# Clearing block buffers between weight casts, reordering chunk loads, moving the first casts to VectorE and taking four turns of q and k one product later in a fused retention and gated feed-forward kernel

## The chip, the cores and the metric

The kernel runs on one core of a Trainium2 chip. The metric is the device time of one execution in microseconds (us), the median of several executions. The profile's span is shorter than that time by about 1.8 us (335.2 against 336.99 us for the profiled execution of the kernel before). Engines are named as in the profile: PE (TensorE), PEld (its weight loads), DVE (VectorE), ACT (ScalarE), POOL (GpSimd), SP (the queue that issues the DMAs).

## The reference

```python
scores = scale * np.matmul(q, k.transpose(0, 1, 3, 2))      # batch 8, heads 8, sequence 576, head 64
Dmat = np.where(rel >= 0, gamma[:, None, None] ** rel[None, :, :], 0.0)
ret = scores * Dmat[None, :, :, :]
attn = np.matmul(ret, v)
x = attn.transpose(0, 2, 1, 3).reshape(B * S, H * D)        # 4608 tokens x 512
out = (sigmoid(x @ w_gate) * (x @ w_val)) @ w_out           # hidden 1536
```

The decay splits into a factor for the row and a factor for the column. The kernel multiplies q and k by tables of these while it casts them to bf16, and carries a running state from chunk to chunk.

## The kernel before

TensorE interleaves the retention with the feed-forward products. The first 768 columns (tokens) are done in three "pairs" of 128-row tiles; the rest is done in chunks of up to 128 rows. For a chunk, the loads are cast into buffers in block-diagonal form (zeros must surround the blocks, so each of the four buffers of each kind, `qk_nat` and `vbd`, is cleared once), and a DMA transpose turns q and k:

```python
for nm, src in (("v", v), ("k", k), ("q", q)):        # load(s): order of the three loads of a chunk
    ...
def casts_to(s):
    while done["cast"] <= min(NS - 1, s):
        x = done["cast"]
        loads_to(x + (1 if x < 12 else 2))
        cast_k(x)      # GpSimd: 4 instructions of 64x256, into qk_nat
        cast_q(x)      # GpSimd: 1 instruction of 128x512, into qk_nat
        cross(x)       # DMA transpose of qk_nat, issued by SP
        cast_v(x)      # GpSimd: 4 instructions of 64x256, into vbd
        done["cast"] += 1
```

The loads, the transposes and the stores all go through one queue, in program order. The middle of the kernel, where the weights' casts end and the chunks begin (cuts marked):

```python
    for i in range(4):
        cast_w("g", 4, 4, i, on_pool)
    step(h_both((2, 3)), 4)                 # gate and value products of feature blocks 2, 3
    ...                                     # casts and products of blocks 4 to 7, casts of 8 to 11
    for t in vbd[0:2]:
        nc.gpsimd.memset(t, 0.0)
    ...                                     # casts of w_out and of the third pair's k, q
    units = h_both((8, 9, 10, 11))
    step(units, 4)
    turn("k", 2, 0, tr_psum, "tr")          # TensorE transposes a block of k or q; ScalarE copies it out
    step(units, 1)
    cast_wo(3, on_act)
    turn("q", 2, 0, pv_psum, "pv")
    ...
    pair_qk(2, 0, QK)
    op_first((0, 1, 2), (0,), opps)         # output products
    pair_qk(2, 1, [(tr_psum, "tr"), (pv_psum, "pv")])
    nc.vector.memset(qk_nat[0], 0.0)
    nc.vector.memset(qk_nat[1], 0.0)
    op_first((0, 1, 2), (1, 2), opps)
    later_constants()                       # the causal mask, GpSimd
    ...
    for t in vbd[2:4]:
        nc.gpsimd.memset(t, 0.0)
    for t in qk_nat[2:4]:
        nc.vector.memset(t, 0.0)
    casts_to(1)
```

## Time and profile before

| | before |
|---|---|
| median | 337.68 us (336.75 to 338.0, 3 runs; a fourth came with the result) |
| span, granted clock | 335.2 us, 1.000 |
| PE busy | 325.7 us |
| GpSimd, ScalarE, VectorE busy | 186.4, 167.6, 165.1 us |

Busy times say who works; the chain says what the end depends on. The page gives the chain that ended last as shares of the span, by engine:

```profile
PE 76%; DMA 10%; POOL 8%; issue 2%; SPq 1%; DVE 1%; ACT 1%; POOLq 0%; DVEq 0%
```

TensorE is 97% busy and yet only 76% of this chain. For the rest, the end hangs on DMAs and on GpSimd. In order of time, the chain leaves TensorE at 25.4 us and comes back to it at 84.42 us, and no row of TensorE stands in between (cuts marked):

```profile
26.41 5.31 DMA wv<-in_moe_w_val_dram
...
40.12 5.95 DMA wo<-in_moe_w_out_dram
46.12 0.62 POOL wo_sb L230
...
79.58 4.80 DMA T<-qk_nat
84.42 0.41 PE qk L410 x8
```

So TensorE's waits between 26 and 84 us don't lie on this chain; the one at 84.42 us does.

### The profile page before, as it was taken

To read this page: it belongs to the slowest core of one execution; us is meant where nothing else is said; L and a number is where in the kernel's file an instruction comes from. 1 tells how busy PE (TensorE), PEld (TensorE's weight loads), DVE (VectorE), ACT (ScalarE), POOL (GpSimd) and SP (SyncE) were. 2 spreads that over 40 slices of the span, in tenths; PEclk is the share of its full clock that TensorE was granted. 3 is DMA by queue.
4 is the path that set the end of the run, shared out by engine and by line. 5 is a ranking of instruction groups with operands and counts; after the bars stand their busy time and mean duration, and the time that the engine had idled before them with its cause. 6 is when DMAs were issued, how large, how long until landed. Compare 5 with 4: busy or idle time off the path is not lost.

```text
span 335.2 us, 7536 instructions
## 1 busy us (share of the span) xinstructions
PE 325.7 (97%) x2836; PEld 190.0 (57%) x2868; DVE 165.1 (49%) x331; ACT 167.6 (50%) x345; POOL 186.4 (56%) x328
## 2 busy tenths in 40 slices
PE   8899999999999999999999999999999999999996
PEld 7764445969566566556566555545555455444443
DVE  5845755626376356436346635542574156503320
ACT  6555635547566456355556655445646455233321
POOL 5675679868969898882448966582577500000000
PEclk9999999999999999999999999999999999999999
DMA  7999996899999999999986999499765850020002
GB/s 215 315 369 348 341 267 128 164 189 185 189 200 186 205 195 249 188 215 225 248 136 128 192 241 198 99 192 277 143 137 80 254 203 0 2 95 31 2 31 94
DMA packets 164100, 60.00 MB, mean 179 GB/s; under 512 B 144480, under 2 KB 156000, under 8 KB 164064
## 3 DMA queue, kind: packets, MB, share of 16 engines
q1 hardware_dynamic: 163920, 59.39, 82.9%
q8 instruction: 22, 0.36, 0.5%
q10 hardware_dynamic: 144, 0.13, 0.1%
q14 instruction: 14, 0.11, 0.1%
HBM read 37.75 MB, written 9.44 MB: 141 GB/s over the span
## 4 chain that ended last, share of the span: by engine, by line
PE 76%; DMA 10%; POOL 8%; issue 2%; SPq 1%; DVE 1%; ACT 1%; POOLq 0%; DVEq 0%
PE h L506 42%; PE op L572 22%; DMA wo<-in_moe_w_out_dram 3%; POOL qk_nat L258 3%; PE pv L431 2%; PE qk L410 2%; DMA k32p<-in_k_dram 2%; PE pv L429 2%; DMA wv<-in_moe_w_val_dram 2%; DMA k<-in_k_dram 2%; POOL qk_nat L268 2%; PE st L443 1%; POOL vbd L279 1%; DMA T<-qk_nat 1%; SPq L114 1%
## 5 line engine op out<-in xcount | busy, mean ns | idle before, releaser
L506 PE MATMUL h<-xT,wg_sb 128*128 128x384 bf16 (+2 forms) x476 | 102.4, 336 | 0.4 <-DVE gv L534 0.2
L506 PE MATMUL h<-xT,wv_sb 128*128 128x384 bf16 (+2 forms) x473 | 102.2, 336 | 0.4
L258 POOL TENSOR_TENSOR qk_nat<-k,ktab 64x256 bf16<-64x256 f32 x120 | 73.5, 612 | 43.0 <-PE st L443 27.8
L534 DVE TENSOR_TENSOR gv<-g,h 128x384 bf16<-128x384 bf16 (+1 forms) x96 | 59.7, 621 | 72.1 <-PE h L506 55.7
L572 PE MATMUL op<-wo_sb,gv 128*128 128x512 bf16 x356 | 84.5, 379 | 0.8
L530 ACT ACTIVATE g<-h 128x384 bf16<-128x384 f32 (+1 forms) x96 | 52.2, 544 | 64.9 <-PE h L506 58.3
L449 DVE CAST sbd<-st 64x256 bf16<-64x256 f32 x104 | 43.7, 420 | 45.3 <-PE st L443 43.0
L506 PEld LDWEIGHTS <-wg_sb 128*128 128x128 bf16 x480 | 43.7, 98 | 31.4 <-issue 0.4
L506 PEld LDWEIGHTS <-wv_sb 128*128 128x128 bf16 x480 | 44.1, 98 | 29.0 <-issue 0.4
L279 POOL CAST vbd<-v 64x256 bf16<-64x256 f32 x120 | 47.6, 397 | 14.6 <-PE pv L431 6.1
L572 PEld LDWEIGHTS <-gv 128*128 128x128 bf16 x372 | 34.3, 98 | 36.3
L549 ACT COPY ob<-op 128x512 f32<-128x512 f32 x33 | 19.3, 586 | 47.0 <-PE op L572 41.4
L289 ACT CAST vs<-v 64x256 bf16<-64x256 f32 x104 | 41.9, 403 | 1.6
L268 POOL TENSOR_TENSOR qk_nat<-q,qtab 128x512 bf16<-128x512 f32 (+1 forms) x34 | 35.4, 1042 | 2.6
L433 ACT CAST xT<-pv 128x512 bf16<-128x512 f32 (+1 forms) x34 | 18.2, 534 | 18.3 <-PE pv L431 18.2
L412 DVE TENSOR_TENSOR pt<-qk,tri 128x512 bf16<-128x512 f32 (+1 forms) x34 | 21.2, 625 | 6.1 <-PE qk L410 5.8
L443 PEld LDWEIGHTS <-qk_nat 128*128 128x128 bf16 x208 | 13.2, 98 | 8.7
L431 PE MATMUL pv<-pt,vbd 128*128 128x64 bf16 x240 | 18.0, 193 | 0.0
L431 PEld LDWEIGHTS <-vbd 128*128 128x128 bf16 x240 | 15.2, 98 | 3.5
L429 PE MATMUL pv<-T,sbd 128*128 128x64 bf16 x216 | 17.2, 193 | 0.0
L522 DVE TENSOR_TENSOR gv<-g,h 128x256 bf16<-128x256 bf16 x24 | 10.0, 420 | 13.8 <-ACT g L520 13.4
L429 PEld LDWEIGHTS <-sbd 128*128 128x128 bf16 x216 | 15.1, 98 | 2.5
(80 smaller groups left out, 238.3 us busy)
## 6 DMA issues: line engine op xcount, KB each, us to landing
out_dram<-ob SPq DMA_DIRECT2D x34, 256.0 KB, 2.9
v<-in_v_dram SPq DMA_DIRECT2D x26, 256.0 KB, 4.1
k<-in_k_dram SPq DMA_DIRECT2D x26, 256.0 KB, 4.6
q<-in_q_dram SPq DMA_DIRECT2D x26, 256.0 KB, 5.0
wg<-in_moe_w_gate_dram SPq DMA_DIRECT2D x12, 256.0 KB, 5.8
wv<-in_moe_w_val_dram SPq DMA_DIRECT2D x12, 256.0 KB, 5.4
wo<-in_moe_w_out_dram SPq DMA_DIRECT2D x12, 256.0 KB, 5.4
k32p<-in_k_dram SPq DMA_DIRECT2D x6, 256.0 KB, 5.4
```

What stands on the lines that cost most here:

```text
L258: nc.gpsimd.tensor_tensor(out=kn[half(hh), j, :, half(hh)], in0=k32[half(j), hh::2, :], in1=ktab[half(j), c, hh::2].unsqueeze(2).to_broadc ...
L268: nc.gpsimd.tensor_tensor(out=qs[0:n], in0=q32[0:n], in1=qtab[0:n, c, :].unsqueeze(2).to_broadcast([n, H, D]), op=ALU.mult)
L279: nc.gpsimd.tensor_copy(out=vb[half(hh), j, :, half(hh)], in_=v32[half(j), hh::2, :])
L289: nc.scalar.copy(out=natural["vs", s][half(hh), j], in_=loaded[s][0][half(j), hh::2, :])
L412: nc.vector.tensor_tensor(out=pt[:, :, 0:n].rearrange("p m (j t) -> p m j t", t=64), in0=qkp[:, :, 0:n].rearrange("p m (j t) -> p m j t", ...
L429: nc.tensor.matmul(pvp[:, m, half(j)], lhsT=before[:, m, :], rhs=qT[:, m, half(j)], start=True, stop=False)
L431: nc.tensor.matmul(pvp[:, m, half(j)], lhsT=vb[:, j, m, :], rhs=pt[:, m, half(j)], start=before is None, stop=True)
L449: nc.vector.tensor_copy(out=sb[half(hh), :, half(hh)], in_=st_tiles[b][half(hh)])
L506: nc.tensor.matmul(out, lhsT=w_sb[:, kc, fc * P:(fc + 1) * P], rhs=xT[:, kc, t0 + a:t0 + e], start=(kc == 0), stop=(kc == NKC - 1))
L530: nc.scalar.activation(out=g[:, 0:n], in_=h1[:, 0:n], func=AF.Sigmoid)
L534: nc.vector.tensor_tensor(out=gvs[some[0]][:, a:e], in0=g[:, 0:n], in1=h2[:, 0:n], op=ALU.mult)
L572: nc.tensor.matmul(opp, lhsT=gvs[fc][:, nb * P:(nb + 1) * P], rhs=wo_sb[:, fc, :], start=(fc == 0), stop=(fc == NFC - 1))
```

## The change

The intent is to take work off GpSimd in the stretch where the first chunk's transpose is being prepared, and to stop two short waits of TensorE on the third pair's turns (a turn is a TensorE transpose of a block of q or k). It has three parts, called turns, clears and casts below:

```diff
 # casts: load order, and the first casts on VectorE
-        for nm, src in (("v", v), ("k", k), ("q", q)):
+        for nm, src in (("k", k), ("q", q), ("v", v)):
...
-            cast_q(x)
+            cast_q(x, nc.vector if x < 2 else nc.gpsimd)
             cross(x)
-            cast_v(x)
+            cast_v(x, on_dve if x == 0 else on_pool)
...
+    casts_to(0)
     cast_dense(0, 0)
 # clears: between the weight casts
+    later_constants()
     for i in range(4):
         cast_w("g", 4, 4, i, on_pool)
+    nc.gpsimd.memset(vbd[0], 0.0)
...                                  (vbd[1], vbd[2], qk_nat[0:3] likewise, further on)
-    for t in vbd[0:2]:
-        nc.gpsimd.memset(t, 0.0)
...                                  (the later clears and later_constants go)
 # turns: one product later, and one output product ahead of the first scores
     step(units, 4)
     cast_wo(2, on_pool)
+    step(units, 1)
     turn("k", 2, 0, tr_psum, "tr")
+    cast_wo(3, on_act)
     step(units, 1)
-    cast_wo(3, on_act)
     turn("q", 2, 0, pv_psum, "pv")
...
+    op_first((0,), (0,), opps)
     pair_qk(2, 0, QK)
-    op_first((0, 1, 2), (0,), opps)
+    op_first((1, 2), (0,), opps)
     pair_qk(2, 1, [(tr_psum, "tr"), (pv_psum, "pv")])
-    nc.vector.memset(qk_nat[0], 0.0)
-    nc.vector.memset(qk_nat[1], 0.0)
+    nc.vector.memset(qk_nat[3], 0.0)
+    nc.gpsimd.memset(vbd[3], 0.0)
```

More of the change, by code (lines that the diff above doesn't have):

```diff
@@ L253, in cast_k @@
         n = width[c]
-        k32 = loaded[s][1]
+        k32 = loaded[s][0]
         kn = qk_nat[s % NB][:, 1:3]
@@ L261, in cast_k, with cast_q, cast_v @@
         natural["k", s] = kn
-    def cast_q(s):
+    def cast_q(s, eng=nc.gpsimd):
         b, c = STEPS[s]
         n = width[c]
-        q32 = loaded[s][2]
+        q32 = loaded[s][1]
         qs = qk_nat[s % NB][:, 0].rearrange("p m (hh d) -> p (m hh) d", d=D)
-        nc.gpsimd.tensor_tensor(out=qs[0:n], in0=q32[0:n],
-                                in1=qtab[0:n, c, :].unsqueeze(2).to_broadcast([n, H, D]), op=ALU.mult)
-    def cast_v(s):
+        eng.tensor_tensor(out=qs[0:n], in0=q32[0:n],
+                          in1=qtab[0:n, c, :].unsqueeze(2).to_broadcast([n, H, D]), op=ALU.mult)
+    def cast_v(s, eng=on_pool):
         b, c = STEPS[s]
         n = width[c]
-        v32 = loaded[s][0]
+        v32 = loaded[s][2]
         vb = vbd[s % NB]
@@ L278, in cast_v @@
             for hh in range(2):
-                nc.gpsimd.tensor_copy(out=vb[half(hh), j, :, half(hh)], in_=v32[half(j), hh::2, :])
+                eng(out=vb[half(hh), j, :, half(hh)], in_=v32[half(j), hh::2, :])
         natural["vb", s] = vb
@@ L288, in cast_dense @@
         for hh in range(2):
-            nc.scalar.copy(out=natural["vs", s][half(hh), j], in_=loaded[s][0][half(j), hh::2, :])
+            nc.scalar.copy(out=natural["vs", s][half(hh), j], in_=loaded[s][2][half(j), hh::2, :])
     def cross(s):
@@ L740 @@
     cast_w("v", 4, 4, 3, on_dve)
+    nc.gpsimd.memset(vbd[1], 0.0)
     units = h_both((4, 5, 6, 7))
+    for t in qk_nat[0:2]:
+        nc.vector.memset(t, 0.0)
     step(units, 4)
@@ L746 @@
     cast_w("g", 8, 4, 3, on_act)
+    nc.gpsimd.memset(vbd[2], 0.0)
     step(units, 4)
@@ L757 @@
     cast_wo(1, on_dve)
+    nc.vector.memset(qk_nat[2], 0.0)
     cast_pair("q", 2, 0, nc.vector)
@@ L762 @@
     cast_wo(2, on_pool)
+    step(units, 1)
     turn("k", 2, 0, tr_psum, "tr")
+    cast_wo(3, on_act)
     step(units, 1)
-    cast_wo(3, on_act)
     turn("q", 2, 0, pv_psum, "pv")
+    cast_wo(4, on_pool)
     step(units, 1)
-    cast_wo(4, on_pool)
     turn("k", 2, 1, tr_psum, "tr")
@@ L771 @@
     turn("q", 2, 1, pv_psum, "pv")
-    step(units, 1)
     cast_wo(5, on_act)
@@ L790 @@
     opps = [ffn_psum.tile([P, 512], FP32, tag="ffn", name=f"op_0_{nb}") for nb in range(3)]
+    op_first((0,), (0,), opps)
     pair_qk(2, 0, QK)
-    op_first((0, 1, 2), (0,), opps)
+    op_first((1, 2), (0,), opps)
     pair_qk(2, 1, [(tr_psum, "tr"), (pv_psum, "pv")])
-    nc.vector.memset(qk_nat[0], 0.0)
-    nc.vector.memset(qk_nat[1], 0.0)
+    nc.vector.memset(qk_nat[3], 0.0)
+    nc.gpsimd.memset(vbd[3], 0.0)
     op_first((0, 1, 2), (1, 2), opps)
-    later_constants()
     op_first((3, 4, 5), range(3), opps)
@@ L821 @@
     store(opps[3], 3 * P, on_act)
-    for t in vbd[2:4]:
-        nc.gpsimd.memset(t, 0.0)
-    for t in qk_nat[2:4]:
-        nc.vector.memset(t, 0.0)
     casts_to(1)
```

## The prediction

> **What bounds the kernel now.** I read the shares of busy time first, then the list of what TensorE (PE) waited for, then PE's instructions in order of time around each wait, and last what VectorE (DVE), GpSimd (POOL) and the DMA issues did just before those waits.
>
> The page of the kernel before, busy time:
>
> ```profile
> span 335.2 us, 7536 instructions
> PE 325.7 (97%) x2836; PEld 190.0 (57%) x2868; DVE 165.1 (49%) x331; ACT 167.6 (50%) x345; POOL 186.4 (56%) x328
> ```
>
> PE is short of work for 335.2 - 325.7 = 9.5 us only. Its list of waits says which of that is a wait (us in total, times, longest):
>
> ```profile
> PE kTp L317 <- POOL kp L248: 1.0, 3, 0.4
> PE qk L410 <- DMA T<-qk_nat: 0.6, 2, 0.4
> PE st L351 <- ACT sbd L362: 0.6, 1, 0.6
> PE qTp L317 <- ACT qT L327: 0.4, 1, 0.4
> ```
>
> The change touches the first, second and fourth. In order of time (start, length, and in brackets the idle time that the view shows) they are these, each below the row ahead of it:
>
> ```profile
> 32.15 3.62 PE L621 MATMUL hg<-xT,wg_sb 128*128 128x512 bf16 x15
> 36.15 0.40 PE L317 MATMUL kTp<-ident,kp 128*128 128x128 bf16 x4 [0.39 <-POOL kp L248]
> ...
> 38.55 1.03 PE L621 MATMUL hv<-xT,wv_sb 128*128 128x512 bf16 x4
> 39.98 0.38 PE L317 MATMUL qTp<-ident,qp 128*128 128x128 bf16 x4 [0.40 <-ACT qT L327]
> ...
> 56.05 0.60 PE L506 MATMUL h<-xT,wv_sb 128*128 128x256 bf16 x4
> 57.08 0.41 PE L410 MATMUL qk<-T 128*128 128x64 bf16 x8 [0.43 <-DMA T<-qk_nat]
> ...
> 83.61 0.60 PE L506 MATMUL h<-xT,wv_sb 128*128 128x256 bf16 x4
> 84.42 0.41 PE L410 MATMUL qk<-T 128*128 128x64 bf16 x8 [0.21 <-DMA T<-qk_nat]
> ```
>
> The brackets understate the loss, because a row's length includes the drain of its last product, which a following product would overlap. From start to start, sixteen 512-column products take 3.45 us elsewhere (rows at 25.24 and 28.69), four take 0.86, four 256-column ones 0.435. So PE should have gone on at 32.15 + 3.45 = 35.60, 38.55 + 0.86 = 39.41, 56.05 + 0.435 = 56.49 and 83.61 + 0.435 = 84.05. It lost 0.55, 0.57, 0.59 and 0.37 us: **2.08 us in all**. These are the four places that the change can win. From 84.9 to 320 us PE shows only one more wait that is named, 0.2 us at 178.6 on a VectorE product; gaps of 0.05 "issue" are records that are missing.
>
> Why the third wait is there, from GpSimd's and the DMA queue's order of time:
>
> ```profile
> 46.12 0.62 POOL L230 CAST wo_sb<-wo 128x512 bf16<-128x512 f32 x1 [0.86 <-DMA wo<-in_moe_w_out_dram]
> 46.68 0.15 POOL L212 MEMSET tri<- 128x64 bf16 x1
> 46.90 0.52 POOL L214 TENSOR_SCALAR_AFFINE_SELECT tri<-tri 64x64 bf16<-64x64 bf16 x2
> 47.48 1.84 POOL L823 MEMSET vbd<- 128x1024 bf16 x2
> 49.41 2.66 POOL L258 TENSOR_TENSOR qk_nat<-k,ktab 64x256 bf16<-64x256 f32 x4
> 52.14 1.04 POOL L268 TENSOR_TENSOR qk_nat<-q,qtab 128x512 bf16<-128x512 f32 x1
> 53.21 1.54 SPq L295 DMA_TRANSPOSE T<-qk_nat  x1
> ```
>
> GpSimd runs without a pause from 46.12: mask, two memsets, k, q. Then the transpose goes out at 53.21 and lands 3.8 us later (that tile's view), at 57.0, where PE stands. The fourth wait is the same chain some chunks on (a k load landing, GpSimd casting to 79.5, a transpose issued at 79.58 that lands after 4.8).
>
> **What the Trainium skill says.** "Perfetto Trace Analysis", section "Identifying the Most-Contended Engine", warns that matmul busy share is no measure of headroom. The trace agrees in part: busy ends are longer than the starts' spacing (1.03 against 0.86 us above), so I used spacing. "TensorE: Matmul & The Clock Gate", "Back-to-back issue gap", gives about N/2.4 + 2.5 ns for one isolated product and 131 ns in a sustained stream at N=512. This trace has 3.45/16 = 216 ns and agrees with the isolated form, so PE is streaming at its rate and only waits can be won. "VectorE: DVE Perf Modes", "Zero memsets can be issued as uint32 (trn2)", counts one cycle per element; the buffer clears are indeed 128x768 uint32 here, 0.70 us each. "SBUF — State Buffer", "SBUF: two separate sides", says that VectorE and GpSimd lock a shared pair of ports for whole instructions. The trace fits: a VectorE weight cast at 33.17 takes up to 1.28 us, beside a GpSimd memset, against 0.43 for the same form at 27.04.
>
> **The change part by part.** No product and no byte is added or removed; PE's work stays the same.
>
> *Clears between weight casts.* GpSimd's three vbd clears (0.92 us each, half of 1.84) and the mask (0.15 + 0.52 = 0.67) go to 22 to 31 us. There GpSimd waits 0.7 to 0.8 us before most casts for weights to land, so they mostly fill idle time. By my replay from the landing times (issue time plus time to landing), the second v weight cast of feature blocks 4 to 7 ends at about 27.2 instead of 27.0, and PE's use of it starts at 28.69; the later casts catch up by 31 us. After the last w_out cast (46.74) only one clear is left, so k can start at 46.7 + 0.9 = 47.7 instead of 49.4.
>
> *VectorE.* Two qk_nat clears (1.4 us) fall between 27.5 and 29.0, where VectorE idles 2.36 us before 29.82; the third falls at about 34.3 to 35.0, ahead of a q load that lands at 35.6. All are hidden. The clears at 53.2 (1.50) go away, which pays for the casts that VectorE takes over.
>
> *Turns one product later.* The k turn now comes after the first v product, at 35.60 + 0.86 = 36.46, and k is ready at 36.10 (start 34.88 + 1.22): the 0.55 is gone. The ScalarE copy that frees the bank for the last q turn still stands behind a w_out cast that waits for its DMA: 38.68 + 0.62 = 39.30, + 0.73 = about 40.0. PE comes to that turn after three more products and three turns of about 0.3: 36.46 + 3 x 0.86 + 3 x 0.3 = 39.9. So the 0.57 shrinks to about 0.1. The next wait could be the pair's second half of scores, which needs that last turn copied (two copies, to about 41.3); I put PE there at 41.3, since one output product has been moved ahead of the first half. I allow 0.1 more. **Gain about 0.9 us.**
>
> *k, q, v and VectorE's casts.* k takes the slot in which v was issued (40.83 + 6.3 = 47.1), q the next (41.54 + 6.8 = 48.3), v the third (42.45 + 7.0 = 49.5). GpSimd casts k from 47.7 to 50.4. VectorE casts q after its last state copy (before at 49.78, about 0.9 earlier now), so 49.3 to about 50.2, at 0.75 to 1.04 for that form. The transpose leaves at 50.4 instead of 53.2 and lands at about 54.2 to 54.8; PE comes to it at 56.49 - 0.9 = 55.6. **The 0.59 is gone.** The second chunk's transpose moves from 58.75 to about 53.5, and its followers stand in the same queue, so the transpose of 79.58 should leave some 4 to 5 us earlier; its wait of 0.37 has gone even if PE is 1.5 us ahead. **Gain 0.37.**
>
> Sum: 0.9 + 0.59 + 0.37 = 1.86 us. Span 335.2 - 1.9 = 333.3.
>
> **The rivals.**
> *VectorE becomes the wait.* q (1.0), four v copies (0.3 to 0.4 each, an estimate from the 0.43 of a cast of twice the size and the 0.42 of one of this size from PSUM) and then the output copies stand in order before the product of the next block needs its bank at 53.7. I get 49.3 + 1.0 + 1.4 = 51.7 and the copy at 52.4, so 1.3 us of room. If port locks with GpSimd's k casts double these, 0.3 to 1 us comes back: 336.0 to 336.7.
> *The earlier casts are held up by the loads.* If the second k lands late (50.7), GpSimd idles 0.3 us before it. It eats slack, not time. If the loads themselves slide because a clear delays a buffer's release, the w_out casts would slide with them; in the compiled order each load waits for the landing of the one eight before it, landings come 0.68 us apart from 25 to 32 us, and the clears fit in GpSimd's idle time between them, so I give this little weight: +0.5 us.
> *More than the sum.* The whole of PE's idle time inside the run is under 6 us when head and tail are left out, so even a perfect version gains under 2%. A large gain is ruled out.
>
> **Range and chances.** The three times before are 336.75 to 338.0; the profiled run took 336.99 for its span of 335.2. Their mean of 337.5 less 1.9 is 335.6. With 0.5 us of noise on a median and the rivals above, 334.3 to 337.0 should hold it 8 times in 10. Faster by over 2% would need 6.8 us, more than three times what the waits hold: 0.01. Slower by over 2% would need a new stall of over 8 us, which no view suggests: 0.01. Within 2%: 0.98.
>
> **What would show it.** Right: PE's list of waits has no kTp after 30 us, no qk wait on the transposes, qTp under 0.2; the first transpose leaves near 50.4, and the last block's products start 1.5 to 2.1 us earlier. Wrong: a new wait of PE on a weight cast between 24 and 36 us (clears too costly), on an output copy near 54 us (VectorE overloaded), on op after the turns, or a transpose wait that is still there near 55 or 83 us.

## The result, and the profile after

The changed kernel takes 335.13 us (334.9 to 335.28, 4 runs), beside 337.25 us (336.75 to 338.0, 4 runs) for the kernel before. The ratio is 0.9935, with a 95% interval of 0.9912 to 0.9958. A ratio here compares the fast runs of both kernels, so it isn't quite the ratio of the medians that are quoted. It is a gain of about 2.1 us that stands clear of the noise.

The page of the changed kernel, its span, its busy times and its chain:

```profile
span 333.2 us, 7536 instructions
PE 325.4 (98%) x2836; PEld 191.4 (57%) x2868; DVE 168.2 (50%) x337; ACT 167.4 (50%) x345; POOL 184.1 (55%) x322
...
PE 94%; DMA 1%; issue 1%; ACT 1%; DVE 1%; SPq 0%; DVEq 0%
```

TensorE's own work is the same. The chain has changed: TensorE is now 94% of it, and DMAs and GpSimd, 18% before, are down to about 1%. TensorE's list of waits (us in total, times, longest) has lost the transposes and the third pair's k turn; the short waits that it still shows on qkp and qTp stand at 6 to 12 us, in the first pairs:

```profile
PE st L351 <- ACT sbd L362: 0.7, 1, 0.7
PE qkp L336 <- ACT qT L327: 0.4, 2, 0.3
PE op L792 <- issue: 0.3, 2, 0.2
PE h L506 <- DVE gv L534: 0.2, 1, 0.2
PE qTp L317 <- DVE qp L248: 0.2, 1, 0.2
```

The four places of the prediction, in order of time (start, length; a bracket would follow if there were idle time of 0.15 us or more):

```profile
36.45 0.39 PE L317 MATMUL kTp<-ident,kp 128*128 128x128 bf16 x4
...
39.76 0.38 PE L317 MATMUL qTp<-ident,qp 128*128 128x128 bf16 x4
...
55.40 0.40 PE L410 MATMUL qk<-T 128*128 128x64 bf16 x8
...
82.36 0.40 PE L410 MATMUL qk<-T 128*128 128x64 bf16 x8
```

No row has a bracket. (From start to start the last turn of q still lost 0.06 us: the product ahead of it starts at 38.84 and four take 0.86. A row's length can't be used for this, as it runs past the start of the next row: 28.68 and 3.62 make 32.30, and the next starts at 32.13.) And the hand-over to the first transpose, from the order of time of GpSimd, VectorE and the DMA queue:

```profile
47.30 0.95 POOL L801 MEMSET vbd<- 128x1024 bf16 x1
48.21 5.73 POOL L258 TENSOR_TENSOR qk_nat<-k,ktab 64x256 bf16<-64x256 f32 x8
...
49.02 1.03 DVE L268 TENSOR_TENSOR qk_nat<-q,qtab 128x512 bf16<-128x512 f32 x1
50.05 2.67 DVE L279 CAST vbd<-v 64x256 bf16<-64x256 f32 x4
52.76 1.29 DVE L549 COPY ob<-op 128x512 f32<-128x512 f32 x2
...
51.25 2.18 SPq L295 DMA_TRANSPOSE T<-qk_nat  x1
```

The transpose leaves at 51.25 instead of 53.21 and lands 3.9 us later, at 55.1. TensorE stands there at 55.40, so only 0.3 us of room is left.

A ledger that leaves out the first 20 us or so, which vary from execution to execution, helps from here on. The **head** is the time until TensorE's first 512-column product starts. The **body** runs from there to the start of the last product. Before: 21.79 and 309.89 us. After: 21.77 and 307.83 us. The body got 2.06 us shorter; the four waits had been counted at 2.08.

### The profile page after: what moved, and what is told of

Its sections match the earlier page's. It is cut to its first block, busy times and chain, and to the rows that moved or that the text cites. A ratio compares the mean times of both kernels' runs of the same rounds, so it can differ in the third digit from the quotient of the medians.

```text
span 333.2 us, 7536 instructions
## 1 busy us (share of the span) xinstructions
PE 325.4 (98%) x2836; PEld 191.4 (57%) x2868; DVE 168.2 (50%) x337; ACT 167.4 (50%) x345; POOL 184.1 (55%) x322
## 4 chain that ended last, share of the span: by engine, by line
PE 94%; DMA 1%; issue 1%; ACT 1%; DVE 1%; SPq 0%; DVEq 0%
PE h L506 49%; PE op L572 24%; PE op L792 3%; PE hv L621 3%; PE hg L621 3%; PE pv L431 2%; PE qk L410 2%; PE pv L429 2%; PE st L443 2%; DMA q32p<-in_q_dram 1%; PE op L562 1%; PE idle L166 1%; PE pvp L382 1%; PE qkp L336 1%; PE hg L700 1%
## 5 line engine op out<-in xcount | busy, mean ns | idle before, releaser
L279 POOL CAST vbd<-v 64x256 bf16<-64x256 f32 x116 | 46.4, 400 | 16.4 <-PE pv L431 11.9
L268 POOL TENSOR_TENSOR qk_nat<-q,qtab 128x512 bf16<-128x512 f32 (+1 forms) x32 | 33.3, 1042 | 2.5
```

Source lines behind the costliest of these rows:

```text
L268: eng.tensor_tensor(out=qs[0:n], in0=q32[0:n], in1=qtab[0:n, c, :].unsqueeze(2).to_broadcast([n, H, D]), op=ALU.mult)
L279: eng(out=vb[half(hh), j, :, half(hh)], in_=v32[half(j), hh::2, :])
```

## The experiments

All twelve runs gave correct results; one of them, after_again, is the changed kernel once more. Each was timed in five rounds beside the kernel before on its chip. "Lowest" is the fastest single run; those of the kernel before were 336.38 us beside the first four, 336.54 beside the next four, 337.1 beside v_twice and op_back, and 337.08 beside the last two.

| run | median (lowest), us | median of before beside it | ratio, 95% interval | head | body |
|---|---|---|---|---|---|
| turns_only | 337.45 (336.6) | 337.83 | 1.0008, 0.9985 to 1.0031 | 22.07 | 310.22 |
| clears_only | 337.18 (335.99) | 337.83 | 0.9994, 0.997 to 1.0017 | 23.83 | 308.59 |
| casts_only | 337.36 (336.18) | 337.83 | 1.001, 0.9979 to 1.004 | 25.39 | 308.36 |
| after_again | 335.7 (334.87) | 337.83 | 0.9941, 0.9921 to 0.9961 | 25.59 | 307.77 |
| no_turns | 335.73 (335.5) | 337.38 | 0.9947, 0.9927 to 0.9968 | 21.97 | 308.43 |
| turns_clears | 336.4 (335.64) | 337.38 | 0.9965, 0.9943 to 0.9987 | 23.55 | 307.78 |
| pool_casts | 335.35 (334.67) | 337.38 | 0.9949, 0.9919 to 0.9978 | 21.46 | 307.93 |
| old_order | 335.55 (334.99) | 337.38 | 0.9946, 0.9919 to 0.9974 | 22.08 | 308.21 |
| v_twice | 335.43 (334.74) | 338.19 | 0.9932, 0.9899 to 0.9966 | 23.11 | 307.77 |
| op_back | 335.43 (334.95) | 338.19 | 0.9934, 0.9901 to 0.9967 | 21.80 | 307.87 |
| after_dense | 334.82 (334.32) | 338.19 | 0.9905, 0.9886 to 0.9925 | 22.70 | 307.17 |
| pool_dense | 334.81 (334.64) | 338.19 | 0.9926, 0.9895 to 0.9958 | 22.19 | 307.17 |

One warning on the last two columns. They come from one profiled execution each, and its head varied from 21.46 to 25.59 us. Where the head is late, TensorE comes late to the transposes, which don't all wait for it, and a wait that an execution with an early head would have shows as none. So a body of 307.8 with a head of 23 us doesn't prove that the wait is gone.

### turns_only

```diff
 # kernel before, the part "turns" alone
+    step(units, 1)
     turn("k", 2, 0, tr_psum, "tr")
...                                  (the other turns and the output product, as in the change)
```

> The kernel before with only the turns of the third pair moved one product later (and one output product ahead of the first scores). My theory: TensorE's two waits at 35 and 39 us (0.55 and 0.57) go, but the first block transpose still lands at about 57.0 and the later one at about 84.4, because neither chain touches TensorE; so the first transpose wait grows from 0.59 to about 1.7 us, what is won is lost again, and the span stays at 335.2 within 0.3 (ratio to before 0.999 to 1.001). Rival, the parts simply add: 1.1 us faster, ratio about 0.9967.

The ratio is 1.0008 (0.9985 to 1.0031): no gain is seen, and the rival of 1.1 us is out. TensorE reached the new block's first product 0.80 us sooner, counted from the first 512-column product (54.10 - 22.07 against 54.62 - 21.79), and then lost it all again. The two transposes' places in TensorE's order of time:

```profile
57.43 0.41 PE L410 MATMUL qk<-T 128*128 128x64 bf16 x8 [1.30 <-DMA T<-qk_nat]
...
85.03 0.41 PE L410 MATMUL qk<-T 128*128 128x64 bf16 x8 [0.48 <-DMA T<-qk_nat]
```

The brackets were 0.43 and 0.21 before; from start to start the waits are 1.47 and 0.64 us, against 0.59 and 0.37. The clearest sign is the time from the landing of the second of these transposes to the start of the last product: 331.68 - 84.38 = 247.30 us in the kernel before, and 332.29 - 84.99 = 247.30 us here. TensorE waits for that landing in both, so the end is pinned to it, and what TensorE won ahead of the first transpose is lost. The first transpose, for its part, left 7.15 us after the last w_out load had landed, in both kernels (46.07 and 53.21; 46.45 and 53.59).

### clears_only

```diff
 # kernel before, the part "clears" alone
+    nc.gpsimd.memset(vbd[0], 0.0)       # and so on, between the weight casts
```

> The kernel before with only the clears and the mask moved between the weight casts. My theory: GpSimd starts k at 48.2 to 48.9 instead of 49.4, so the first transpose leaves at about 52.5 and lands at about 56.3, ahead of TensorE at 56.5; the wait at 57 goes (0.5 to 0.6 us) and the one at 84 shrinks from 0.37 to about 0.2: 0.6 to 0.9 us faster, ratio about 0.998. Rival, the clears between casts cost as much as they save (weight casts late, new waits of TensorE between 24 and 36 us): 0, or slower.

The gain is 0.2 us by the mean, 0.4 us by the lowest runs (335.99 against 336.38), and the interval includes none. So this came out smaller than I expected. GpSimd's order of time shows why:

```profile
47.30 0.95 POOL L800 MEMSET vbd<- 128x1024 bf16 x1
49.32 2.65 POOL L258 TENSOR_TENSOR qk_nat<-k,ktab 64x256 bf16<-64x256 f32 x4 [1.06 <-DMA k<-in_k_dram]
```

GpSimd was free at 48.25 and then waited 1.06 us for k, because v had been loaded ahead of it. The first transpose left 6.42 us after the last w_out load instead of 7.15, and the two after it were 0.7 us sooner too, but the later transpose that TensorE waits for was not (33.62 us after that load, against 33.51 before). Ahead of it GpSimd waited for the fifth chunk's k load, which took 6.0 us to land (64.81 to 70.83) against 5.2 before (64.86 to 70.09). (The bracket there names a TensorE product, but GpSimd starts 0.16 us after the landing in both profiles.) This is one profile; whether the clears have to do with that load isn't shown. The end stayed pinned: 332.42 - 85.12 = 247.30 us once more. The rival, new waits on late weight casts, didn't show: TensorE's list has none between 24 and 36 us. This profile had a late head (23.83), so the wait at the first transpose can't be read from it. What the clears alone are worth is taken up again under after_again.

### casts_only

```diff
 # kernel before, the part "casts" alone
-        for nm, src in (("v", v), ("k", k), ("q", q)):
+        for nm, src in (("k", k), ("q", q), ("v", v)):
...                                  (and the first casts on VectorE, casts_to(0) early, as in the change)
```

> The kernel before with only the load order k, q, v and the first casts on VectorE (the first chunk's casts ahead of the dense copies, as in the change). My theory: k starts at about 47.5, the first transpose leaves near 51 and lands near 55, so the wait at 57 goes (0.59); the late clears now stand in front of the second chunk's casts on both engines, so the wait at 84 goes only in part, and VectorE's first gate products come late: 0.4 to 0.9 us faster, ratio 0.9973 to 0.9988. Rival, VectorE is overloaded here, where it still has its clears: a new wait of TensorE of 0.5 us or more on VectorE after 54 us, no gain.

No gain by the mean (1.001, a wide interval), 0.2 us by the lowest runs. The profile has no wait on a transpose, but TensorE stands twice on VectorE's gate products, at 60.37 and 61.59 us, 0.30 and 0.24 us from start to start. They stand behind q, v, the output copies and the clears, which are still there. This is the rival: two waits of about half its 0.5 us, 0.54 together. The profile's head was very late (25.39), and VectorE's q cast stands behind a state copy that waits for TensorE, so the transpose left at 53.33 rather than near 51. What the part is worth with an early head stays open; that it brings the 2 us alone is unlikely by the times (see after_again).

### after_again

> The whole change again, beside the parts on the same chip: ratio to before about 0.9938, that is 2.0 to 2.1 us faster; all four waits gone. If the parts add without interplay, the gains of the three parts sum to this; by my theory the turns alone give nothing, and the sum of the three falls short by about 0.6 to 1 us.

The unchanged changed kernel, on the same chip as the three parts. The ratio is 0.9941, so 2.0 us, while the three parts alone gave 1.0008, 0.9994 and 1.001. Taken as they stand, those three sum to no gain. But they can't be taken so. Two of the six executions of each part had a mean granted clock of 0.990 to 0.995 and took 337.72 to 339.59 us, while all eleven of the kernel before beside them had 0.999 or more; and 0.9941 is what comes out when the changed kernel's one such execution, 338.64, is left out (335.52 over 337.50). The parts need not be to blame: the kernel before had such executions too, four of eleven beside v_twice and five of eleven beside after_dense.

With the executions at 0.999 or more alone, the means are 337.50 us before, 337.20 for the turns, 336.75 for the clears, 336.95 for the casts and 335.52 for the whole change. That is 0.3, 0.75 and 0.55 us, in sum 1.6, against 2.0. By the lowest runs the sum is 0.4 against 1.5. Four executions of one part spread over 1.0 to 1.4 us, so these sums can't decide between parts that add up and the shortfall of 0.6 to 1 us that I expected. **That the whole is worth 2 us is clear; whether the parts add up to it isn't settled.** What the traces do show is that the turns' gain was lost at the transposes (turns_only).

The profiled execution was the slow one (338.64 us); the reason is in its windows (the stretch and its length, busy us and instructions of PE, PEld, DVE, ACT and POOL, then the granted clock, the DMA share and GB/s):

```profile
17.00:24.00 7.00, 7.00 (x90) 5.23 (x89) 2.23 (x4) 3.00 (x9) 5.94 (x12) 0.51 1.04 357
```

The clock was granted at half for 6.8 us from 17.1 us on, and the head ended at 25.59 instead of 21.77. The body was 307.77, as in the other profile of this kernel.

### no_turns

```diff
 # changed kernel, turns back where they were
-    step(units, 1)
     turn("k", 2, 0, tr_psum, "tr")
...                                  (the other turns and the output product back too)
```

> The changed kernel with the turns put back where they were. My theory: the two waits of 0.55 and 0.57 come back near 36 and 40 us and nothing else, since the transposes now land early: 1.0 to 1.1 us slower than the changed kernel, 1.0 us faster than before (ratio 0.997). So the turns are worth 1.1 here and nothing in the kernel before. Rival, the turns never mattered: as fast as the changed kernel (ratio 0.994).

The body is 308.43, so 0.6 us longer than the changed kernel's, and the lowest run is 0.63 us above that kernel's 334.87 (on another chip; by the ratios, 0.9947 and 0.9941, it is only 0.2). Of the two waits only one came back:

```profile
39.71 0.39 PE L317 MATMUL qTp<-ident,qp 128*128 128x128 bf16 x4 [0.50 <-ACT qT L327]
```

From start to start that is 0.67 us. The wait on GpSimd's k cast did not come back: the turn started at 35.78 right behind its product. With the clears gone from in front of it, GpSimd's k cast ran at 34.55 for 1.04 us in this run, as in the changed kernel (against 34.88 and 1.22 before), so it was ready at 35.59, before the turn came at 35.78. So the clears removed that wait already, and the turns are worth about 0.6 us by the profile in the changed kernel, not 1.1. In the kernel before no gain from them is seen.

### turns_clears

```diff
 # changed kernel without "casts": v, k, q again, all casts on GpSimd, casts_to(0) not early
```

> The changed kernel without the load order and without casts on VectorE (turns and clears only). My theory: k lands second and GpSimd casts k and q one after the other, so the first transpose leaves at about 52.7 and lands at about 56.5, where TensorE stands from 55.4: a wait of about 1.1 us, and about 0.3 at the later transpose; 0.6 to 0.9 us faster than before (ratio about 0.998). Rival, clearing early is enough and the rest is decoration: 2 us faster (0.994).

The ratio is 0.9965, so 1.2 us faster than before, and the lowest run is 0.8 us above the changed kernel's lowest. That lies between the two theories, nearer to mine by the lowest runs; "clearing early is enough" is out. The profile had a head of 23.55 us and so shows no wait. Its transpose left 6.11 us after the last w_out load, as against 4.56 in the changed kernel; with a head of 21.8 us TensorE would have been there 0.5 us before it landed (55.4 against 55.89; an estimate from the two profiles). So the lost 0.8 us is shown by the times, and a wait on the transpose as its cause is likely but in no trace.

### pool_casts

```diff
 # changed kernel
-            cast_q(x, nc.vector if x < 2 else nc.gpsimd)
+            cast_q(x)
-            cast_v(x, on_dve if x == 0 else on_pool)
+            cast_v(x)
```

> The changed kernel with q of the first two chunks and v of the first cast by GpSimd again; the load order k, q, v stays. My theory: k from 48.2 to 50.9, q to 51.9, the transpose leaves at 52.0 and lands at about 55.9, TensorE waits about 0.5 us at 55.4 and up to 0.3 at the later one: 0.5 to 0.8 us slower than the changed kernel (ratio to before about 0.9955). Rival, the casts on VectorE only move work (GpSimd has slack and port locks slow both): as fast as the changed kernel.

My theory fell. The kernel is as fast as the changed one: lowest run 334.67, and a body of 307.93 with the earliest head of all (21.46), so this reading is not blurred. GpSimd's order of time:

```profile
47.04 2.65 POOL L258 TENSOR_TENSOR qk_nat<-k,ktab 64x256 bf16<-64x256 f32 x4
49.77 1.04 POOL L268 TENSOR_TENSOR qk_nat<-q,qtab 128x512 bf16<-128x512 f32 x1
```

q took GpSimd 1.04 us, and VectorE 1.03 in the changed kernel's profile, though 0.67 or 0.68 in the six other profiles with this cast on VectorE and the new order. The transpose left 5.32 us after the last w_out load here and 4.56 us after it in the changed kernel. Against the other runs with the casts on VectorE (4.83 to 5.03 in op_back, no_turns and v_twice) it is 0.3 to 0.5. So VectorE does save 0.3 to 0.8 us there, but they are slack. This load had also landed 1.2 us earlier in this execution (45.52 against 46.69).

### old_order

```diff
 # changed kernel
-        for nm, src in (("k", k), ("q", q), ("v", v)):
+        for nm, src in (("v", v), ("k", k), ("q", q)):
```

> The changed kernel with the chunks loaded v, k, q again. My theory: k lands about 1.1 us later (48.8 for 47.7), GpSimd starts it at 48.9 for 48.2, the first transpose lands at about 55.5 to 55.8, a wait of 0.1 to 0.4 us at 55.4; later transposes have about 2 us of slack: 0.1 to 0.4 us slower than the changed kernel (ratio to before about 0.9945). Rival, the order is the main lever of the change: 0.6 us slower or more. Other rival, it does nothing: equal within 0.1 us.

The lowest run is 0.1 us above the changed kernel's, the body 0.4 us longer, of which 0.38 is a wait on the q turn (at 40.45 us, ahead of the chunks' transposes). So the order is not the main lever where VectorE shares the casts. The second transpose chain shows what it does: the transpose that had been late left 31.29 us after the last w_out load with the old order, 28.23 with the new, and 33.51 before. Both are early enough.

### v_twice

```diff
 # changed kernel
-            cast_v(x, on_dve if x == 0 else on_pool)
+            cast_v(x, on_dve if x < 2 else on_pool)
```

> The changed kernel with the second chunk's v cast on VectorE too, the suspected load doubled. In the changed kernel the four v copies took 2.67 us there beside GpSimd's k casts. My theory: four more copies (1.8 to 2.7 us) stand ahead of the first gate product of the new block, which moves from 55.1 to about 57.5, and TensorE waits for its bank: a wait on VectorE of 1 to 1.6 us near 57 us, 1.0 to 1.6 us slower than the changed kernel. So VectorE is close to its limit with one v. Rival, it has room: no slower than 0.2 us.

My theory fell here too: the lowest run is 334.74 and there is no new wait. VectorE's order of time shows the first chunk's four copies and the second's:

```profile
50.91 2.74 DVE L279 CAST vbd<-v 64x256 bf16<-64x256 f32 x4
...
55.62 1.24 DVE L279 CAST vbd<-v 64x256 bf16<-64x256 f32 x4
```

The same four instructions took 2.74 us while GpSimd cast k (48.66 to 54.86) and 1.24 us while GpSimd stood idle for a load (54.86 to 57.57). The Trainium skill, "SBUF — State Buffer", section "Who interferes with whom", says that VectorE's copies and casts in a two-port mode and GpSimd lock a shared pair of ports and that the one that comes second is blocked. This run agrees in that the copies beside GpSimd's work were slower, and gives a size: a factor of 2.2. (That the lock is what slows them is the page's word; no run varies it.) I had reckoned the second v at the first's price. So VectorE's first gate product ended at 57.31, about 0.5 us before the bank was asked for at 57.8 (the changed kernel's 2.97 us from the new block's first product to its fourth, laid onto this profile).

### op_back

```diff
 # changed kernel
-    op_first((0,), (0,), opps)
     pair_qk(2, 0, QK)
-    op_first((1, 2), (0,), opps)
+    op_first((0, 1, 2), (0,), opps)
```

> The changed kernel with the one output product put back behind the first half of the third pair's scores. The same work lies between the last turn and the second half of the scores either way, so I now expect no difference (within 0.1 us, ratio to before 0.994). What the prediction said of it, that the moved product covers the copy of the last turn, would show as a wait of 0.2 us or more on ScalarE's copy near 40.5 us.

No difference: lowest 334.95 against 334.87, body 307.87 against 307.83, no wait on ScalarE's copy at 40 to 41 us. That one line of the change does nothing that shows.

### after_dense and pool_dense

The traces keep one named wait of TensorE behind the head, at 177 us, in every kernel so far (0.21 shown, 0.38 from start to start). ScalarE's order of time in the changed kernel says why: the copy of the outputs, which waits for TensorE, and two dense copies of the next v stand ahead of the gates.

```profile
172.54 0.59 ACT L433 CAST xT<-pv 128x512 bf16<-128x512 f32 x1 [0.63 <-PE pv L431]
173.14 0.82 ACT L289 CAST vs<-v 64x256 bf16<-64x256 f32 x2
173.98 1.11 ACT L530 ACTIVATE g<-h 128x384 bf16<-128x384 f32 x2
```

The dense copies need nothing of TensorE, so they can fill those 0.63 us:

```diff
 # both; pool_dense also has the first casts back on GpSimd, as pool_casts
         elif kind == "pv":
+            cast_dense(s + 1, 1)
             phase_pv(s)
-            cast_dense(s + 1, 1)
```

> The changed kernel with ScalarE's dense copies of the next chunk's v put ahead of the copy of the outputs (they wait for nothing then, while that copy waits for TensorE). It aims at the one named wait that the changed kernel keeps after 20 us, 0.2 us shown (0.38 from start to start) near 177 us: there two dense copies (0.82) stand before the gate that TensorE's bank needs. My theory: the gate comes 0.6 us earlier and that wait goes; nothing else moves: 0.3 to 0.4 us faster than the changed kernel (lowest time about 334.5 where that kernel's lowest was 334.87). Rival: the outputs' copy comes later elsewhere and new waits of 0.1 to 0.4 us appear.

> The same, with the first q and v casts back on GpSimd: beside the run before it on the same chip this tells once more whether VectorE's casts are worth anything. From the runs so far the first transpose leaves 4.6 to 5.0 us after the last w_out load lands with the casts on VectorE, and 5.3 after it with them on GpSimd (7.1 in the kernel before). My theory now: about 0.5 us of slack is all that they buy; a wait of TensorE on the first transpose appears only if that load lands after about 46.3 us and TensorE is on time; medians within 0.3 us of each other. Rival (as first expected): 0.5 to 0.8 us slower.

Both profiles have lost that wait, and no wait has come in its place; the bodies are both 307.17, so 0.6 us shorter than the changed kernel's, more than the 0.38 of the wait. The remainder is the same place in two earlier chunks: in the changed kernel a group of products beside those gates starts 0.12 us late each time (123.95 and 131.50, where 384-column products otherwise follow every 0.65 us), too short for a bracket, and in after_dense it doesn't. With 0.05 us ahead of the new block that makes 0.66. after_dense has the lowest run and ratio: 334.82 us, lowest 334.32, ratio to before 0.9905 (0.9886 to 0.9925). It beats the kernel before clearly, and the changed one by about 0.5 us by the lowest runs (on another chip).

Beside each other on one chip the two differ by nothing (334.82 and 334.81). The first transpose left 4.70 and 5.32 us after the last w_out load, as in the earlier runs. That load landed at 46.31 in pool_dense, and its transpose landed at 55.41 with TensorE there at 55.77, so even there 0.4 us was left. By the times, VectorE's share in the casts is slack. An execution with a later load and an early head could still wait: laid onto op_back's profile (load at 46.72, TensorE there at 55.47), 5.32 us to leave and 3.8 to land make 55.84, an estimated wait of 0.4 us. No run here has it.

## Why the prediction was right

**The time.** 335.6 was predicted, 335.13 measured, within 334.3 to 337.0. The sum was 1.86 us of four waits that hold 2.08; the body got 2.06 us shorter, and all four waits are gone. The span was to be 333.3 and was 333.2. (One wait is misplaced by the working: the named one at "178.6" stands at 179.16 in TensorE's rows; VectorE's product that ends it starts at 178.64. Nothing hangs on it.)

**Clears between weight casts.** Right in the numbers that can be set beside the trace. The second v weight cast ended at 26.99 (predicted 27.2), VectorE's clears ran from 27.38 to 28.89 and from 34.22 to 34.92 (27.5 to 29.0, 34.3 to 35.0), and TensorE had no wait there. k started at 48.21 instead of 47.7, because the last w_out load landed at 46.69 in that execution instead of 46.07. Over all profiles it landed at 46.07 to 46.45 in the three without early clears and at 45.52 to 47.15 in the eleven with them, so the rival that clears delay the loads isn't borne out.

**Turns.** 0.9 was predicted, and the new block's first product came at 53.54 instead of 54.62: 1.08. The 0.1 that I left for the last q turn was 0.06 in this profile and 0.3 to 0.4 in two others (turns_only, old_order), since ScalarE's copy stands behind a w_out cast that waits for its DMA. The remark that the output product moved ahead of the scores gives room wasn't borne out: op_back showed no effect.

**Transposes.** Predicted to leave at 50.4 and to land at 54.2 to 54.8, before TensorE at 55.6; measured 51.25, 55.1 and 55.40. The later one was to leave 4 to 5 us sooner: 74.92 instead of 79.58. The second chunk's transpose was a miss: put at about 53.5, it left at 55.69, since its q cast stood behind v and two output copies on VectorE and ended at 54.94, and the queue was still issuing loads until 55.57.

**VectorE as the new wait.** The slowdown that this rival put down to locks is real. The four v copies took 2.67 us where I had put 1.4, and the output copy came at 52.76 instead of the 51.7 at which I had put its start. There was still room, and it cost nothing.

**What failed in the working, though the sum was right.** All four waits went, so their sum had to come out; the credit given to each part did not. First, the prediction read "gain about 0.9 us" for the turns and 0.59 and 0.37 for the transposes as amounts that stand by themselves. In the kernel before, the end was pinned to the landing of the later transpose (247.30 us ahead of the last product in three kernels), so the turns alone brought nothing that shows. The chain had said this: between 25.4 and 84.42 us it runs over DMAs and GpSimd and not over TensorE, and of the four waits only the last lies on it. Second, it put the 0.59 down to "k, q, v and VectorE's casts". The order of loads or VectorE's casts, either with the clears, is enough to make the transposes early (pool_casts, old_order); with neither, about 0.8 us of the 2 is lost (turns_clears). Third, the 0.55 at the k turn goes with the clears already (no_turns).

**What stays open.** What the clears and the casts are worth each alone, and so whether the three parts add up to the whole.

## What to carry to other kernels

When an engine is 97% busy, list its waits from start to start and add them up: here 2.08 us were counted and 2.06 won. The list isn't a strict bound, since waits under 0.15 us carry no bracket (after_dense won 0.66 us where 0.38 was named). Then look at the chain before you credit a part with its wait: where the end is pinned to a later landing, a wait removed ahead of it can simply make the later one longer, as the turns alone did. Before you compare small parts by their means, look at the clock of each execution: two at a lower clock in six moved a part's mean by up to 0.8 us here. Work that waits for nothing was moved ahead of instructions that wait (clears, dense copies), and neither move brought a new wait.

## What the Trainium skill lacked or had wrong

- "TensorE: Matmul & The Clock Gate", "Back-to-back issue gap", gives 131 ns in a sustained stream of 512-column products with weight loads. Here sixteen took 3.45 us, 216 ns each, in long streams with a weight load for each, in the kernels before and after (rows at 25.24 and 28.69 before, 25.22 and 28.68 after). Its figure for the isolated product (about 216) is the one that holds.
- The same page, "HAM oscillation — how this bites in real kernels", ties the return of the slow clock to idle gaps above about 3.4 us; its next section also names frequent short idles, for a loop over PSUM banks. Neither lets one foresee what happened here: three of fourteen profiles had the clock at half for 3.4 us (clears_only) or 6.8 us (casts_only, after_again) from about 17 us on, though TensorE's longest named wait there was 0.8 to 1.0 us. Two others with a wait of 1.0 us there did not, and the density ahead of it doesn't tell them apart either: from 10 to 17 us TensorE was busy for 5.14 us in after_again, and for 5.13 in v_twice and 5.11 in after_dense, whose clock stayed whole. The cause stays open. In after_again the head came 3.8 us later than in the other profile of that kernel, more than the change is worth.
- "SBUF — State Buffer", "Who interferes with whom", describes the lock but gives no size for small casts beside GpSimd's multiplications: four 64x256 casts took 2.67 to 2.75 us beside them and 1.24 us without (v_twice).
- "VectorE: DVE Perf Modes", "Zero memsets can be issued as uint32 (trn2)", counts one cycle per element, which with the page's 0.96 GHz is an estimated 0.80 us for 768 elements. Two clears in a row start 0.81 us apart here (27.38 and 28.19), so the count holds; what the section doesn't say is that the record of each is 0.70 us long, so that the length of a row understates its cost.
